# A fixed turn for TensorE between the convolution backward and the weight-gradient jobs, with reloads ahead of transposes and the spectrum's halves swapped on VectorE

## The chip, the cores and the metric

The kernel runs on one core of one Trainium2 chip. The metric is the device time of one execution in microseconds, the median of several runs. The profile is of one further execution; its clock starts at the span's first instruction. A core has a TensorE (matmuls and transposes, results to PSUM), a VectorE, a ScalarE and a GpSimd, each with its own instruction order that is fixed when the program is built, and DMA queues that are fed from the Sync, Scalar and GpSimd sequencers. An engine executes its instructions in order: one that waits holds up all behind it.

## The reference: forward and backward of two interleaved layers

The computation is the forward pass and all gradients of a stack of four residual blocks, A B A B, on 2048 tokens of width 448. A is an H3-style block (a short shift convolution of k, a product with v, a long convolution by FFT, a gate), B is a dense block with silu. Cut to what matters:

```python
def _A_ref(q, k, v, shift_k, ssm_k, ssm_D):
    k_shift = sum over t of k_pad[:, t:t+S] * shift_k[:, ks-1-t]     # 4 taps
    kv = k_shift * v
    kv_f = rfft2(kv padded to 2S);  kf_f = rfft2(ssm_k padded to 2S)
    y = irfft2(kv_f * kf_f)[:S] + kv * ssm_D
    return q * y

def _B_ref(x, w1, w2):
    h = silu(einsum("bsd,df->bsf", x, w1))            # 448 -> 1792
    return einsum("bsf,fd->bsd", h, w2)               # 1792 -> 448

x = A_q
x = x + _A_ref(_layernorm(x), A_k, A_v, ...)
x = x + _B_ref(_layernorm(x), B_w1, B_w2)
x = x + _A_ref(_layernorm(x), A_k, A_v, ...)
x = x + _B_ref(_layernorm(x), B_w1, B_w2)
# outputs: x, and the gradients of q, k, v, shift_k, ssm_k, ssm_D, w1, w2 for a given grad_out
```

Both A blocks share k, v and the convolution, so y is computed once (a prefix), and its gradient once (a suffix).

## The kernel before

The program has three parts. The prefix (to about 105 us) computes the long convolution. `Main` (to about 550 us) goes through the tokens in four chunks of 512: forward of layer 0, forward and backward of layer 1, backward of layer 0. The suffix does the backward of the convolution by FFT (stage 1, transposes `ps_tr`, a second stage `ps_s2`, products with the stored spectra, an inverse stage `ps_v`, then `ps_gK` and `ps_gkv`), and the weight gradients as "jobs": each job is 16 matmuls that accumulate `ps_d` from one loaded tile `dstat` of 512 KB. 28 jobs on activations make the gradient of w2 (`_gw2`), 28 on GH make that of w1 (`_gw1`).

A scheduler places the instructions of each engine; `issue_after` puts an instruction behind a given one. In the trace a tile's buffer number is left out (`ps_s` for `ps_s1` and `ps_s2`), and the copies of `_copy` have lines 111 (ScalarE) and 113 (VectorE).

The parts of `Main` that the change and the prediction touch:

```python
def store_turned(self, dst, tile_, c, hh, groups=((0, 4), (4, 7))):
    self.flush()
    an = self.td.tile([P, NF // 2, 4, P], BF16, name="turned", tag="S", bufs=2)
    for lo, hi in groups:
        nc.sync.dma_start_transpose(out=an[:, lo:hi]..., in_=tile_[:, lo:hi, :]...)       # L484
    self.late = lambda: nc.sync.dma_start(out=dst[...], in_=an[:, lo:hi])                 # L486
...
def slope(self, d):                                                                       # L560
    for o in range(0, 7, 2):
        self.nc.scalar.activation(d[:, o:o + n, :], d[:, o:o + n, :], ACT.Derivative_silu)
...
def ga(self, c, L, gT, dT, mid=None):
    ghT = [self.td.tile([P, NF // 2, 512], BF16, name=f"ghT{h}", tag="T", bufs=3) for h in range(2)]
    for fp in range(NF // 2):
        ps = k.psum.tile([P, 2, 512], FP32, name="ps_g", tag="mm", bufs=2)
        self.contract(ps, self.w2T, gT, 2 * fp, 2, ...)                                   # 8 matmuls, L518
        if fp == 2 and mid:
            mid()
        gh = self.ch.tile([P, 2, 512], BF16, name="ghp", tag="ghp", bufs=1)
        k.last_gh = nc.scalar.copy(gh[:], ps[:])                                          # L625
        ...
            nc.vector.tensor_tensor(out=ghT[hh][...], in0=dT[hh][1][...], in1=gh[...], op=ALU.mult)   # L630
        if fp in (3, 6):
            hh = (fp - 3) // 3
            self.store_turned(k.GH_d[L], ghT[hh], c, hh)
    return ghT
...
def load_d(self, c, hh):                                                                  # L690
    t = self.td.tile([P, NF // 2, 512], BF16, name="dTl", tag="D", bufs=3)
    k.d_load = nc.sync.dma_start(out=t[:], in_=k.DT_d[c, hh])
    return t
...
# run(), backward of layer 0
for c in range(4):
    with self.tc.issue_after(k.mid_u.ins):
        self.slope(d1)
    dT, (nb, na), (gb, gT) = ((None, d0), (None, d1)), nl, gn
    ghT = self.ga(c, 0, gT, dT, (lambda: self.slope(e0)) if c < 3 else None)
    if c < 3:
        d0, d1 = e0, self.load_d(c + 1, 1)
        if c < 2:
            e0 = self.load_d(c + 2, 0)
        gn = self.g_pre(c + 1, 0)
    self.gn(c, 0, ghT, nb, ..., na)          # 4 x 14 matmuls ps_n, then the layer norm's backward on VectorE
```

The parts of the suffix:

```python
k.M1sb = sp0.tile([P, 16, 2, P], BF16, name="M1s", tag="kk0")
with tc.high_priority():
    nc.gpsimd.dma_start(out=k.M1sb[:]..., in_=k.m1_h.ap())
...
_load_minv(k, nc.gpsimd)
for n2 in range(16):
    _fft_stage1(k, n2, k.gYb[:, n2, :], A1, psum)        # 2 matmuls ps_s, one eviction
for g in range(7):
    for i in range(16):
        nc.tensor.transpose(pt[:, i, :], A1f[:, 16 * g + i, :], k.ident[:])               # ps_tr
    _copy(nc, bal.pick(2048, dve_ns=0.53), Z[...], pt[:])

def spectrum(cp):                                         # cp: a pair of chunks of 1024 columns, 7 in all
    kk = (sp0.tile(..., name="kk_c", tag="kk0") if cp % 2 else p1.tile(..., name="kk_c", tag="kk1"))
    xsw = p1.tile([P, 2048], BF16, name="xsw_c", tag="xsw", bufs=2)
    nc.gpsimd.dma_start(out=t[0], in_=k.SPEC_d["K"][:, lo:hi])
    nc.gpsimd.dma_start(out=t[1], in_=k.SPEC_d["KV"][:, lo:hi])
    ...
    for u in range(2):
        # 2 matmuls ps_s, 512 columns each; then the eviction into Zf
    _swap_halves_dma(k, t[2], Zf, lo, hi, nc.scalar, dlo=0)      # L245, L246: two DMAs of 64 partitions

def inverse(cp, t):                                       # 4 times per cp: 2 products, 16 matmuls ps_v, an eviction
    nc.vector.tensor_tensor(out=pa[:], in0=Zf[...], in1=spec_t[:, o], op=ALU.mult)
    nc.vector.tensor_tensor(out=pb[:], in0=t[2][:, o], in1=spec_t[:, o], op=ALU.mult)
    _fft_inv_stage2_chunk(...)
...
slots = [(k.dp, "dstat", 3)]
with tc.issue_after(k.go_jobs.ins):
    _gw2(k, k.dp, range(4), slots)
slots = [(k.dp, "dstat", 3), (k.dp, "dstat", 3), (dp2, "dstat", 2), (k.dp, "dstat", 3), (dp2, "dstat", 2)]
_gw2(k, k.dp, range(4, NF), slots)
_gw1(k, dp2, slots, k.mov3, mov1)
```

The jobs are written last; the scheduler pulls their matmuls forward between those of the convolution wherever it takes TensorE to be free, so the turn in which the two kinds stand is the scheduler's.

Of the kernel before, what the change touches and what calls it, by code (L numbers as in the profile page):

```python
# [17 lines left out]
P = 128  # L18
# [188 lines left out]

def _fft_stage1(k, n2, rhs, A1, psum):
    nc = k.nc
    ps = psum.tile([P, 2, 512], FP32, name="ps_s1", **k.pt["s1"])  # L210
    for c in range(2):
        nc.tensor.matmul(ps[:, c, :D], lhsT=k.M1sb[:, n2, c, :], rhs=rhs, start=True, stop=True)
    _copy(nc, k.bal.pick(2 * D), A1[:, :, :, n2, :].rearrange("p dh c ds -> p c dh ds"), ps[:, :, :D].rearrange("p c (dh ds) -> p c dh ds", ds=4))

# [249 lines left out]
class Main:  # L464
# [98 lines left out]
    def h(self, c, L, nT, half, hold):  # L563
# [3 lines left out]
        hold.append((aT, dT))  # L567
        for ft0, n, at in ((0, 2, 1), (2, 2, 0), (4, 2, None), (6, 1, None)) if half == 0 else ((7, 1, None), (8, 2, 1), (10, 2, 0), (12, 2, None)):
# [20 lines left out]
        if L == 1:  # L589
            self.store_turned(k.A_d[1], aT, c, half)  # L590

# [24 lines left out]
    def ga(self, c, L, gT, dT, mid=None):  # L616
        nc, k = self.nc, self.k
        ghT = [self.td.tile([P, NF // 2, 512], BF16, name=f"ghT{h}", tag="T", bufs=3) for h in range(2)]
        for fp in range(NF // 2):
            ps = k.psum.tile([P, 2, 512], FP32, name="ps_g", tag="mm", bufs=2)  # L620
            self.contract(ps, self.w2T, gT, 2 * fp, 2, None if fp == 6 else (fp + 1) % 2)
            if fp == 2 and mid:
                mid()
# [3 lines left out]
            k.bal.add("dve", -0.5)  # L627
            for u in ((0, 1),) if fp != 3 else ((0,), (1,)):
# [3 lines left out]
            if fp in (3, 6):  # L632
                hh = (fp - 3) // 3
                self.store_turned(k.GH_d[L], ghT[hh], c, hh)
        return ghT
# [71 lines left out]
    def run(self):  # L707
# [21 lines left out]
        for c in range(4):  # L729
            gb, gT = self.g_pre(c, 1)  # L730
            self.h(c, 1, nT, 1, cur)
# [3 lines left out]
            self.turn_plain(c)  # L735
            if c == 3:
                d0 = self.load_d(0, 0)
                self.slope(d0)
                k.GO = k.wk.tile([P, NT, D], BF16, name="GO", tag="WA")
                with self.tc.issue_after(k.d_load.ins):  # L740
                    nc.sync.dma_start(out=k.GO[:], in_=_pm(k.grad_out[0]))
            box = []
            ghT = self.ga(c, 1, gT, cur, (lambda: box.append(self.b_pre(c + 1, 3))) if c < 3 else None)
# [5 lines left out]
            else:  # L749
                d1, e0 = self.load_d(0, 1), self.load_d(1, 0)  # L750
# [5 lines left out]
        for c in range(4):  # L756
# [3 lines left out]
            ghT = self.ga(c, 0, gT, dT, (lambda: self.slope(e0)) if c < 3 else None)  # L760
            if c < 3:
                d0, d1 = e0, self.load_d(c + 1, 1)
                if c < 2:
                    e0 = self.load_d(c + 2, 0)
                gn = self.g_pre(c + 1, 0)
            self.gn(c, 0, ghT, nb, lambda tl: self.X[:, 4 * c + tl, :], na)
            if c < 3:
                with self.tc.issue_after(k.d_load.ins):
                    nl = self.load_n(c + 1)
        self.flush()  # L770


def _job(k, ps, src, ft, mov, slot, start, stop):
    pl, tag, bufs = slot
    st = pl.tile([P, NT, P], BF16, name="dstat", tag=tag, bufs=bufs)
    k.nc.sync.dma_start(out=st[:], in_=src[:, ft, :, :])
    for t in range(NT):
        i = k.nc.tensor.matmul(ps[:, :D], lhsT=st[:, t, :], rhs=mov[:, t, :], start=start and t == 0, stop=stop and t == NT - 1)  # L778
    return i


def _gw2(k, pool, fts, slots, bufs=2):
    nc = k.nc
    for ft in fts:
        ps = k.psum.tile([P, 512], FP32, name="ps_d", tag="tr", bufs=2)
        for L, mov in ((0, k.X), (1, k.GO)):
            slot = slots.pop(0)
            slots.append(slot)
            _job(k, ps, k.A_d[L], ft, mov, slot, L == 0, L == 1)
# [5 lines left out]
def _gw1(k, pool, slots, mov3, mov1):  # L795
    nc, psum = k.nc, k.psum
    out7v = k.outs[7].rearrange("(c p) f -> p c f", p=DC)

# [9 lines left out]
    for ft in range(NF):  # L808
        ps = psum.tile([P, 512], FP32, name="ps_d", tag="tr", bufs=2)
        for L, mov in ((1, mov3), (0, mov1)):  # L810
            slot = slots.pop(0)
            slots.append(slot)
            i = _job(k, ps, k.GH_d[L], ft, mov, slot, L == 1, L == 0)
            if hold:
                with k.tc.issue_after(i.ins):
                    turn(*hold)
                hold = None
        o = pool.tile([P, D], BF16, name="dout", tag="dout", bufs=2)
        nc.vector.tensor_copy(o[:], ps[:, :D])  # L819
# [4 lines left out]
def _ssm_suffix(k):  # L824
# [7 lines left out]
    with ExitStack() as es:  # L832
        pool = lambda name: es.enter_context(tc.tile_pool(name=name, bufs=1, reuse_waits="tile"))
        sp0 = pool("sp0")
        k.M1sb = sp0.tile([P, 16, 2, P], BF16, name="M1s", tag="kk0")
        with tc.high_priority():
            nc.gpsimd.dma_start(out=k.M1sb[:].rearrange("p a c k -> p (a c k)"), in_=k.m1_h.ap())
        sp = pool("sspec")
        k.Minvsb = sp.tile([P, 16, 2, P], BF16, name="Minvs")
        dp2 = pool("dp2")  # L840
# [190 lines left out]
```

## Time and profile before

| what | value |
|---|---|
| time, median of 3 runs | 794.23 us (793.31 to 805.97) |
| span of the profiled run | 792.3 us |
| VectorE / ScalarE busy | 515.6 / 440.6 us |
| DMA moved | 183.69 MB, mean 232 GB/s |
| last matmul's start, from the trace | 784.8 us |

By stretch of the program, from the windows (busy us of each engine, the granted TensorE clock, 1.00 is full):

| stretch, us | TensorE | VectorE | ScalarE | clock | GB/s |
|---|---|---|---|---|---|
| 0 to 110, prefix | 91.21 | 81.62 | 81.76 | 0.96 | 251 |
| 110 to 365, forward and layer 1 | 248.24 | 182.26 | 172.35 | 1.00 | 223 |
| 365 to 550, end of layer 1, layer 0 backward | 160.66 | 133.69 | 113.07 | 0.94 | 242 |
| 550 to 792, convolution backward and jobs | 224.56 | 118.07 | 73.40 | 0.98 | 225 |

A line of the page's groups reads: line, engine, operation, output <- inputs, shape, count, then busy time, mean length of one in ns, and the idle time before it with what ended it. Matmuls overlap in the engine, so a mean of 350 ns is the time one takes from end to end, and not the pace. A line of a timeline is start, length, engine, source line, what, count, and in brackets the idle time ahead of it with its releaser.

### The profile page before, as it was taken

To read this page: it belongs to the slowest core of one execution; us is meant where nothing else is said; L and a number is where in the kernel's file an instruction comes from. 1 tells how busy PE (TensorE), PEld (TensorE's weight loads), DVE (VectorE), ACT (ScalarE), POOL (GpSimd) and SP (SyncE) were. 2 spreads that over 40 slices of the span, in tenths; PEclk is the share of its full clock that TensorE was granted. 3 is DMA by queue.
4 is the path that set the end of the run, shared out by engine and by line. 5 is a ranking of instruction groups with operands and counts; after the bars stand their busy time and mean duration, and the time that the engine had idled before them with its cause. 6 is when DMAs were issued, how large, how long until landed. Compare 5 with 4: busy or idle time off the path is not lost.

```text
span 792.3 us, 12745 instructions
## 1 busy us (share of the span) xinstructions
PE 724.7 (91%) x5025; PEld 381.3 (48%) x5025; DVE 515.6 (65%) x1056; ACT 440.6 (56%) x551; POOL 101.7 (13%) x169
## 2 busy tenths in 40 slices
PE   6999779999999999999978899996989998999995
PEld 4976534444444434434433343343556674545553
DVE  3789778788435978859457976985365625797110
ACT  4879867766466676876836866633536644000000
POOL 1133212222100010000000000010111022111111
PEclk9999989999999999999998999997989999999998
DMA  9359999999968869889998887995978766587660
GB/s 317 136 158 283 373 258 299 308 249 233 254 173 171 174 185 218 218 174 221 356 266 231 213 239 205 247 195 219 397 223 263 244 266 218 173 307 220 192 179 17
DMA packets 188888, 183.69 MB, mean 232 GB/s; under 512 B 135482, under 2 KB 164030, under 8 KB 187804
## 3 DMA queue, kind: packets, MB, share of 16 engines
q1 hardware_dynamic: 173664, 120.93, 59.2%
q0 software_dynamic: 12832, 53.92, 19.8%
q10 hardware_dynamic: 2332, 8.03, 3.2%
q8 instruction: 39, 0.64, 0.3%
q14 instruction: 21, 0.17, 0.1%
HBM read 76.50 MB, written 65.87 MB: 180 GB/s over the span
## 4 chain that ended last, share of the span: by engine, by line
PE 33%; DVE 21%; issue 20%; ACT 13%; DMA 8%; POOL 3%; SPq 0%; POOLq 0%; DVEq 0%; ACTq 0%
PE ps_h L518 5%; PE ps_d L778 5%; PE ps_o L598 4%; PE ps_g L518 4%; PE ps_n L666 3%; DVE dT L113 3%; DMA dTl<-DT_d 3%; ACT ghp L625 3%; DVE lb_junk L641 2%; DMA kk_c<-spec_KV 2%; DVE lb_u L652 2%; PE ps_v L232 2%; DVE ghT L630 2%; PE ps_v L233 2%; ACT na L274 2%
## 5 line engine op out<-in xcount | busy, mean ns | idle before, releaser
L778 PEld LDWEIGHTS <-dstat 128*128 128x128 bf16 x896 | 87.0, 99 | 87.4 <-issue 8.3
L518 PE MATMUL ps_g<-gT,w2T 128*128 128x512 bf16 (+1 forms) x448 | 100.7, 385 | 17.6 <-ACT ghp L625 17.0
L518 PE MATMUL ps_h<-nT,w1sb 128*128 128x512 bf16 (+1 forms) x448 | 103.9, 385 | 4.7 <-DVE dT L113 2.6
L666 PE MATMUL ps_n<-w1T,ghT 128*128 128x448 bf16 x448 | 94.2, 356 | 0.7 <-ACT lb_u L668 0.2
L598 PE MATMUL ps_o<-w2sb,aT 128*128 128x448 bf16 x448 | 90.8, 353 | 0.8 <-ACT aT L574 0.8
L778 PE MATMUL ps_d<-mov,dstat 128*128 128x448 bf16 x448 | 87.2, 352 | 0.9 <-DMA mov<-N_d 0.9
L574 ACT ACTIVATE aT<-ps_h 128x1024 bf16<-128x1024 f32 (+1 forms) x64 | 58.3, 917 | 37.6 <-PE ps_h L518 28.8
L113 DVE CAST dT<-ps_h 128x1024 bf16<-128x1024 f32 (+1 forms) x56 | 59.3, 1066 | 26.2 <-ACT aT L574 26.1
L518 PEld LDWEIGHTS <-w2T 128*128 128x128 bf16 (+1 forms) x448 | 36.3, 97 | 78.1 <-issue 47.3
L625 ACT CAST ghp<-ps_g 128x1024 bf16<-128x1024 f32 x56 | 56.5, 1008 | 30.6 <-DVE ghT L630 18.5
L518 PEld LDWEIGHTS <-w1sb 128*128 128x128 bf16 (+1 forms) x448 | 36.3, 97 | 68.3 <-issue 40.3
L666 PEld LDWEIGHTS <-ghT 128*128 128x128 bf16 x448 | 42.2, 98 | 45.4 <-issue 4.6
L598 PEld LDWEIGHTS <-aT 128*128 128x128 bf16 x448 | 42.1, 98 | 43.4 <-issue 4.3
L778 PE MATMUL ps_d<-X,dstat 128*128 128x448 bf16 x224 | 54.3, 372 | 5.1 <-DMA dstat<-A_d 5.1
L804 ACT COPY do<-ps_dt 112x512 bf16<-112x512 bf16 x14 | 8.2, 585 | 82.6 <-PE ps_dt L802 82.6
L232 PE MATMUL ps_v<-Gsb,pa 128*128 128x128 bf16 x336 | 43.2, 223 | 10.1 <-DVE Zg L113 5.8
L778 PE MATMUL ps_d<-GO,dstat 128*128 128x448 bf16 x224 | 50.0, 355 | 0.0
L233 PE MATMUL ps_v<-Gsb,pb 128*128 128x128 bf16 x336 | 42.2, 223 | 1.0 <-DVE pb L443 0.7
L819 DVE CAST dout<-ps_d 128x448 bf16<-128x448 f32 x14 | 8.7, 622 | 51.4 <-PE ps_d L778 51.4
L232 PEld LDWEIGHTS <-pa 128*128 128x128 bf16 x336 | 33.5, 100 | 11.7 <-DVE pa L442 6.3
L668 ACT ACTIVATE lb_u<-ps_n,rstd 128x448 f32<-128x448 f32 x32 | 20.2, 632 | 33.4 <-DVE X L653 12.1
L630 DVE TENSOR_TENSOR ghT<-dT,ghp 128x1024 bf16<-128x1024 bf16 (+1 forms) x32 | 19.5, 620 | 27.6 <-ACT ghp L625 27.6
(188 smaller groups left out, 1184.8 us busy)
## 6 DMA issues: line engine op xcount, KB each, us to landing
GH_d<-turned SPq DMA_DIRECT2D x16, 896.0 KB, 6.2
dstat<-A_d SPq DMA_DIRECT2D x28, 512.0 KB, 7.2
dstat<-GH_d SPq DMA_DIRECT2D x28, 512.0 KB, 3.8
A_d<-turned SPq DMA_DIRECT2D x12, 896.0 KB, 4.8
DT_d<-dT POOLq DMA_DIRECT2D x8, 896.0 KB, 6.3
dTl<-DT_d SPq DMA_DIRECT2D x8, 896.0 KB, 6.6
spec_K<-Z POOLq DMA_DIRECT2D x7, 512.0 KB, 7.5
KB<-Z POOLq DMA_DIRECT2D x14, 256.0 KB, 12.3
```

The lines of the kernel that those rows point to most:

```text
L113: eng.tensor_copy(out, in_)
L232: nc.tensor.matmul(pv[:, i, :], lhsT=pa[:, i * P:(i + 1) * P], rhs=k.Gsb[:, ga, :], start=True, stop=False)
L233: nc.tensor.matmul(pv[:, i, :], lhsT=pb[:, i * P:(i + 1) * P], rhs=k.Gsb[:, gb, :], start=False, stop=True)
L274: nc.scalar.activation(n_g[:, tl, :], src(tl), ACT.Identity, bias=nmr[:, tl:tl + 1], scale=r[:, tl:tl + 1])
L518: self.nc.tensor.matmul(ps[:, u, :], lhsT=w[lo:hi, b, f:f + P], rhs=x[lo:hi, b, :], start=(seen[u] == 1), stop=(seen[u] == ND))
L574: last = nc.scalar.activation(a, ps[:, 0:n, :], ACT.Silu)
L598: nc.tensor.matmul(po[:, :D], lhsT=aT[ft // 7][0][:, ft % 7, tl * P:(tl + 1) * P], rhs=self.w2sb[:, ft, :], start=(ft == 0), stop=(ft == N ...
L625: k.last_gh = nc.scalar.copy(gh[:], ps[:])
L630: nc.vector.tensor_tensor(out=ghT[hh][:, o:o + len(u), :], in0=dT[hh][1][:, o:o + len(u), :], in1=gh[:, u[0]:u[0] + len(u), :], op=ALU.mult)
L666: nc.tensor.matmul(pn[:, :D], lhsT=ghT[ft // 7][:, ft % 7, tl * P:(tl + 1) * P], rhs=self.w1T[:, ft, :], start=(ft == 0), stop=(ft == NF - 1))
L668: last_u = nc.scalar.activation(u0[:], pn[:, :D], ACT.Identity, scale=k.rstd[2 * L + 1][:, t:t + 1], accum_out=cp[:, tl, 0:1])
L778: i = k.nc.tensor.matmul(ps[:, :D], lhsT=st[:, t, :], rhs=mov[:, t, :], start=start and t == 0, stop=stop and t == NT - 1)
```

## The change

The change does four things.

1. In the layer backward, the reloads of `dTl` are issued inside `ga`, ahead of the transposes of the same half, where they stood behind those of the whole chunk; the slope of a reloaded tile (`mid`) is placed behind the eviction of the third `ps_g`, where it was free to stand ahead of it. The first reload (`d0`) is issued before the last chunk of layer 1 begins, and the plain transposes of the activations are done two per chunk in the first two chunks.
2. TensorE's turn in the suffix is written out. The jobs become a generator; `_in_turn` chains each group of the convolution's matmuls to the last one placed, and `weave(n)` puts n job matmuls behind it.
3. The loads around it move: M1s into the free slot of w2 by the Sync queue, a chunk earlier; Minv, ksf, gks and mov3 behind the spectrum loads of certain pairs; GO behind the reloads of chunk 0; kk_c gets two buffers of its own. The evictions of the first 12 stage-1 outputs go to ScalarE, and so do those of `_gw1`.
4. The swapped halves of the fresh spectrum are written by two VectorE copies of 64 x 1024 per chunk in place of two DMAs per pair.

No arithmetic is added or taken away. The core of the diff:

```diff
-    def ga(self, c, L, gT, dT, mid=None):
+    def ga(self, c, L, gT, dT, mid=None, loads=(None, None)):
...
-            if fp == 2 and mid:
-                mid()
             gh = self.ch.tile([P, 2, 512], BF16, name="ghp", tag="ghp", bufs=1)
             k.last_gh = nc.scalar.copy(gh[:], ps[:])
+            if fp == 2 and mid:
+                with self.tc.issue_after(k.last_gh.ins):
+                    mid()
...
             if fp in (3, 6):
                 hh = (fp - 3) // 3
+                if loads[hh]:
+                    ld.append(self.load_d(*loads[hh]))
                 self.store_turned(k.GH_d[L], ghT[hh], c, hh)
...
-            ghT = self.ga(c, 0, gT, dT, (lambda: self.slope(e0)) if c < 3 else None)
+            ghT = self.ga(c, 0, gT, dT, (lambda: self.slope(e0)) if c < 3 else None, ((c + 1, 1) if c < 3 else None, (c + 2, 0) if c < 2 else None))
...
+                    if c == 0:
+                        nc.sync.dma_start(out=k.GO[:], in_=_pm(k.grad_out[0]))
+                    if c == 2:
+                        k.M1sb = k.wk.tile([P, 16, 2, P], BF16, name="M1s", tag="WB")
+                        nc.sync.dma_start(out=k.M1sb[:].rearrange("p a c k -> p (a c k)"), in_=k.m1_h.ap())
...
+        def weave(n):
+            with _in_turn(k):
+                for _ in zip(range(n), jobs):
+                    pass
...
         for n2 in range(16):
-            _fft_stage1(k, n2, k.gYb[:, n2, :], A1, psum)
+            with _in_turn(k):
+                _fft_stage1(k, n2, k.gYb[:, n2, :], A1, psum, nc.scalar if n2 < 12 else None)
+            weave(4 if n2 < 8 else 8 if n2 < 11 else 10)
...
+                weave(3)
                 _copy(nc, bal.pick(2048, dve_ns=0.53), Z[:, 16 * g:16 * g + 16, :], pt[:])
...
-                kk = (sp0.tile([P, 2, 2048], BF16, name="kk_c", tag="kk0") if cp % 2 else p1.tile([P, 2, 2048], BF16, name="kk_c", tag="kk1"))
+                kk = p1.tile([P, 2, 2048], BF16, name="kk_c", tag="kk", bufs=2)
...
-                _swap_halves_dma(k, t[2], Zf, lo, hi, nc.scalar, dlo=0)
+                    for q in (0, 64):
+                        nc.vector.tensor_copy(t[2][q:q + 64, u * 1024:(u + 1) * 1024], Zf[64 - q:128 - q, o])
...
-                        _fft_inv_stage2_chunk(k, pa, pb, True, B1, ci, psum, cnd=cnd)
-
+                        with _in_turn(k):
+                            _fft_inv_stage2_chunk(k, pa, pb, True, B1, ci, psum, cnd=cnd)
+                        weave(5)
...
-        _gw2(k, k.dp, range(4, NF), slots)
...
-        _gw1(k, dp2, slots, k.mov3, mov1)
+        weave(2 * NF * 2 * NT)
```

## The prediction

> **What bounds the kernel now.** I read the page first, then TensorE's idle time in the trace, then the waits of the stretches in which it lies. From the page, the busy shares and the clock by slice:
>
> ```profile
> PE 724.7 (91%) x5025; PEld 381.3 (48%) x5025; DVE 515.6 (65%) x1056; ACT 440.6 (56%) x551; POOL 101.7 (13%) x169
> PEclk9999989999999999999998999997989999999998
> ```
>
> TensorE is idle for 792.3 - 724.7 = 67.6 us. The windows give 18.8 of them to the first 110 us, which the change leaves alone, and 6.8 to the 255 us after that, where matmuls run back to back. So what can be won lies in the 42 us of idle time after 365 us, and in matmuls at a slow clock. The dips of the clock row (slices 21, 27, 29) stand where TensorE had stood still. The windows show three holes, and the end for comparison:
>
> ```profile
> 410.00:420.00 10.00, 1.73 (x6) 0.57 (x5) 3.02 (x7) 4.73 (x7) 0.00 (x0) 0.75 1.02 340
> 535.00:545.00 10.00, 3.83 (x13) 1.56 (x13) 3.17 (x9) 3.15 (x5) 0.55 (x1) 0.65 0.91 340
> 570.00:580.00 10.00, 4.74 (x20) 2.12 (x19) 3.03 (x4) 2.43 (x3) 0.55 (x1) 0.78 0.97 332
> 740.00:780.00 40.00, 40.00 (x230) 21.50 (x229) 4.30 (x7) 3.51 (x6) 4.24 (x6) 1.00 0.53 152
> ```
>
> Columns: length, busy PE, PEld, DVE, ACT, POOL, clock, DMA share, GB/s. In each hole every engine is mostly idle and the DMA engines are full: waits for transfers. What TensorE waited for, 355 to 555 us, and ScalarE, 405 to 480 us (us in all, times, longest):
>
> ```profile
> PE ps_g L518 <- ACT ghp L625: 15.1, 8, 8.3
> PE ps_d L778 <- DMA dstat<-A_d: 5.1, 1, 5.1
> PE ps_s L212 <- ACT A1g L111: 1.8, 1, 1.8
> ...
> ACT dTl L560 <- DMA dTl<-DT_d: 12.1, 4, 7.5
> ```
>
> The timelines of ScalarE, then TensorE, then the Sync queue, at the largest hole:
>
> ```profile
> 415.27 1.06 ACT L560 ACTIVATE dTl<-dTl 128x1024 bf16<-128x1024 bf16 x1 [7.46 <-DMA dTl<-DT_d]
> 417.79 1.00 ACT L625 CAST ghp<-ps_g 128x1024 bf16<-128x1024 f32 x1
> ...
> 418.84 3.23 PE L518 MATMUL ps_g<-gT,w2T 128*128 128x512 bf16 x8 [8.27 <-ACT ghp L625]
> ...
> 401.90 7.20 SPq L484 DMA_TRANSPOSE turned<-ghT  x2
> 409.19 0.80 SPq L690 DMA_DIRECT2D dTl<-DT_d  x1
> ```
>
> The reload stands behind two transposes in the Sync queue; the slope (L560) stands ahead of the eviction of ps_g in ScalarE's order; so TensorE waits 8.27 us for a load that it doesn't need yet. The same chain costs 2.51 us at 444 and 1.96 us at 476. The hole at 537 is a dstat load, issued only at 535.5 behind the last GH_d store. The hole at 572 waits for kk_c, which was on its way from 558.9 to 575.4 (chain of waits) while gks, ksf, dstat and kk_c moved together at up to 425 GB/s, and then for the swapped half:
>
> ```profile
> 575.40 1.29 DVE L885 TENSOR_TENSOR pa<-Zg,kk_c 128x1024 bf16<-128x1024 bf16 x2 [5.68 <-DMA kk_c<-spec_KV]
> 581.77 0.69 DVE L886 TENSOR_TENSOR pb<-xsw_c,kk_c 128x1024 bf16<-128x1024 bf16 x1 [3.34 <-DMA xsw_c<-Zg]
> ```
>
> **What the Trainium skill says.** "TensorE: Matmul & The Clock Gate", section "What's actually happening": the array runs at half clock after a window of some 3.4 us with too little work, and returns after a busy one. The trace agrees: granted clock 0.5 for 415.1-422.0, 480.0-483.4, 538.0-548.3 and 575.6-582.4, multiples of 3.41 us, each at a hole; the 8 matmuls above take 3.23 us, 8 others 1.78. A removed hole so returns its length and half of the slow stretch behind it. "VectorE: DVE Perf Modes", section "Side-by-side: where the cycles go for N=2048 bf16": a copy within SBUF in bf16 makes four elements a cycle, with some 150 cycles fixed; by it I estimate 0.43 us for each 64x1024 swap. No copy of that form is in this trace; the nearest, skb<-sk_all with a strided read, takes 1.10. "DMA: Bandwidth & Descriptors", section "Issuing engines are not separate DMA queues": transfers from all issuers share the same 16 engines. It agrees: the swap's 256 KB take 3.0 to 9.6 us, by what else moves.
>
> **The change part by part.** No matmul is added or removed: 5,025 before and after. The pace from start to start is 0.19 us for 448 columns (50 ps_o in 9.69), 0.215 for 512, 0.056 for 128 (27 ps_tr in 1.68).
>
> (a) Slope reloads. In the new order the loads for the next chunks stand ahead of the second transpose of each half, and the slope comes behind the eviction of the third ps_g. Holes of layer 0, as excess over the pace: 8.4 + 2.7 + 0.8 + 0.5 + 2.1 + 0.6 + 0.5 = 15.6 us; half of the slow clock's 3.1 and 3.4 us: 3.3. Together 18.9. Not all comes back: VectorE is busy 97.4 of the 118 us from 418 to 536. Per chunk it has 4 x 5.4 (the lb, G, gy, gYb rows: 2 x 0.70, 2 x 0.17, 0.69, 0.68, 0.76, 2 x 0.38, 2 x 0.39) + 4.9 for ghT = 26.5 us, against some 24.5 on TensorE. VectorE is also idle for nearly all of the first hole, so those 8 to 9 us are real; of the rest I count a third. Gain: 12. The early load of d0 takes perhaps 1 of 2.4 us of gaps at 369-386.
>
> (b) The convolution backward in fixed turn. The last ps_n ends at 527.2, the last matmul starts at 784.8: 257.6 us. The work in it by pace: 835 ps_d x 0.189 = 157.8; ps_s 32 x 0.189 + 28 x 0.215 = 12.1; 744 of 128 columns (ps_tr 112, ps_v 448, ps_gK 128, ps_dt 56) x 0.0565 = 42.0; ps_gkv 6.1; ps_sk and ps_r 5.4; about 80 changes from ps_d to another kind at 0.05 = 4. Sum 227.4, so 30 us are waits and half clock: 2.0 + 5.3 + 3.0 (clock) at 534-548, 5.4 + 2.3 at 572-582, 1.9 at ps_r, 1.1 at mov1, 0.7 + 0.5 + 1.7 in small ones, and some 6 in many tiny ones.
> In the new order 2 ps_s and 4 to 10 ps_d take turns, 106 ps_d before the first ps_tr (79 before), and the evictions of the first 12 stage-1 outputs are on ScalarE, not behind VectorE's late layer norm. M1s is loaded a chunk earlier and Minv later, which frees the DMA engines just when the last ghT transposes gate the next dstat. kk_c no longer shares a slot with M1s, so the first two pairs can come some 20 us before their use.
> What stays: the third ft's dstat is needed 8 x (0.38 + 0.76 + 0.05) = 9.5 us after the last ps_n, and came 15 us after it before; without M1s and Minv I expect 7 to 11, a wait of 0 to 2. mov1 takes 7.8 us against two jobs of 3: 1 to 2. Turn changes rise to some 97: +1. Sum of what stays, with tiny ones: 8. Gain 22.
>
> (c) The swap. 14 DMA pairs go (3.7 MB), 28 VectorE copies come: 28 x 0.43 = 12 us. For a pair of chunks (cp) VectorE then has 8 x 0.69 + 4 x 0.43 = 7.2 us and ScalarE 6 evictions x 1.02 = 6.1, while TensorE has 2 x (0.43 + 0.38) + 4 x (0.90 + 0.95) + turns = 9.7. The copies lie beside TensorE's work: they cost nothing, and the gain is counted in (b).
>
> (d) The end (mov jobs, 7.5 us after the last matmul) is unchanged; dout's eviction moves to ScalarE at 0.54 for VectorE's 0.62. 0.
>
> Sum: 12 + 1 + 22 = 35 us; 794.2 - 35 = 759. As new waits are likelier than forgotten gains I take 761.
>
> **The rivals.** First: the fixed turn makes TensorE wait in place, since a dstat that is late now holds up the spectrum too. Against it: a job of 16 takes 4.5 to 9 us with its neighbours, a dstat lands in 7.2 at the median with three to five slots open. For it: kk_c, dstat, ksf, gks, mov3 and Minv all fall into the 70 us of the spectrum, some 270 GB/s where 244 moved before. If it holds, 8 to 15 us of (b) are lost: 770 to 776.
> Second: VectorE becomes the bound. In layer 0 it nearly is; if only the first hole pays, (a) shrinks to 8: 765. If the swap runs at one element a cycle (1.1 us), a cp costs VectorE 10, just over TensorE's 9.7: again 3 to 5 us.
> Third: GO (1.8 MB), moved into layer 0, and two early plain turns delay reloads or transposes there, so that a hole only moves: 5 us. The gb reload has slack: issued at 279, used at 313.
> Fourth, upward: if VectorE's idle time in layer 0 also goes and tiny waits shrink, 752.
>
> **Range and chances.** Rivals one and two together make some 775, the best case 751: range 751 to 775. Over 2% faster means below 778.3, which asks for 16 of the 35 us; the first hole and the kk_c hole with their clock alone bring nearly that. Faster 0.91, same 0.07, slower 0.02.
>
> **What would show it.** (a): no wait of ps_g for ghp over 1 us, no half clock near 410, the last ps_n 11 to 15 us earlier. (b): last ps_n to last matmul some 235 us, no slow clock in between, no wait for kk_c. (c): swaps at 0.43 us, no idle TensorE behind them. Wrong if ps_d waits for dstat<-A_d in many places, if a slope load again stops ScalarE for over 3 us, or if VectorE is over 90% busy in the spectrum.

## The result and the profile after

The changed kernel takes 768.89 us (median of 4 runs, 765.53 to 771.57), the kernel before, run beside it, 795.23 us. The ratio is 0.9675, 95% interval 0.9621 to 0.9728: 3.25% faster. A second time it was 770.33 us, ratio 0.9754 (0.9716 to 0.9793). The prediction was 761 us, 751 to 775: the time lies in the range, 8 us above the point.

Three marks in the trace, each the start of a matmul, cut the program so that each part of the change can be read by itself: the first `ps_g`, the last `ps_n`, and the last matmul.

| stretch, us | before | after | difference | predicted |
|---|---|---|---|---|
| start to first ps_g (nothing of the prediction) | 232.1 | 234.5 | +2.4 | 0 |
| first ps_g to last ps_n: layers | 294.9 | 284.9 | -10.1 | -13 |
| last ps_n to last matmul: convolution backward and jobs | 257.7 | 242.8 | -14.9 | -22 |
| last matmul to the end | 7.6 | 7.6 | 0.0 | 0 |

The sum is -22.6, from a span of 792.3 to one of 769.8. I call the second stretch "the layers" and the third "the suffix" from here on. The first differs from run to run: 230.4 to 240.6 in the fourteen traces of this study. The two highest values (240.5 and 240.6) come from traces with a wait near 145, where a transposing DMA of aT, 1.5 us in the changed kernel's own trace, took 9.3 and 9.2; the same kernel shows both values, so it is not an effect of the change.

Busy shares and clock by slice, from the page of the changed kernel:

```profile
PE 719.6 (93%) x5025; PEld 382.3 (50%) x5025; DVE 510.3 (66%) x1061; ACT 457.6 (59%) x574; POOL 102.5 (13%) x169
PEclk9999879999999999999999999999999998999999
```

TensorE's idle time fell from 67.6 to 50.2 us, and the three dips that stood behind the middle of the row are gone. One new one stands at 635 to 654 us (the 34th digit). The windows of the changed kernel (length, busy PE, PEld, DVE, ACT, POOL, clock, DMA share, GB/s) show the layers' last stretch, the spectrum, and the two stretches behind it:

```profile
410.00:520.00 110.00, 103.48 (x529) 44.28 (x528) 91.50 (x252) 73.39 (x104) 2.17 (x4) 1.00 1.07 263
562.00:623.00 61.00, 59.67 (x624) 42.23 (x625) 45.27 (x82) 39.49 (x44) 9.29 (x18) 1.00 0.72 264
623.00:646.00 23.00, 20.08 (x183) 14.19 (x181) 2.60 (x3) 8.25 (x9) 5.98 (x9) 0.85 0.74 261
646.00:668.00 22.00, 19.65 (x308) 11.56 (x307) 10.30 (x25) 8.13 (x10) 5.97 (x11) 1.00 0.67 218
```

The spectrum has 1.3 us of idle TensorE in 61. The 45 us behind it have 5.3 us and a slow clock: a part of the suffix where the prediction had seen no large wait. TensorE's waits from 519 to 680 us, the first lines:

```profile
PE ps_gK L981 <- ACT gK L111: 2.9, 1, 2.9
PE ps_sk L1030 <- issue: 2.4, 1, 2.4
PE ps_v L233 <- DVE pb L942: 1.1, 2, 0.8
```

No wait for kk_c, none for a dstat. And in the layers, from 355 to 520 us, the answer to the 15.1 us of before:

```profile
PE ps_g L518 <- ACT ghp L626: 5.4, 12, 1.5
```

### The profile page after: what moved, and what is told of

It is laid out like the page before. It is cut to its first block, busy times and chain, and to the rows that moved or that the text cites. A ratio compares the mean times of both kernels' runs of the same rounds, so it can differ in the third digit from the quotient of the medians.

```text
span 769.8 us, 12724 instructions
## 1 busy us (share of the span) xinstructions
PE 719.6 (93%) x5025; PEld 382.3 (50%) x5025; DVE 510.3 (66%) x1061; ACT 457.6 (59%) x574; POOL 102.5 (13%) x169
## 4 chain that ended last, share of the span: by engine, by line
PE 38%; DVE 25%; issue 15%; ACT 11%; DMA 8%; POOL 3%; SPq 0%; POOLq 0%; DVEq 0%; ACTq 0%
PE ps_d L808 8%; PE ps_o L600 7%; PE ps_h L518 6%; DVE lb_junk L647 3%; DVE dT L113 3%; ACT ghp L626 3%; DVE ghT L634 3%; DVE lb_u L658 2%; DMA turned<-ghT 2%; PE ps_v L233 2%; PE ps_v L232 2%; PE ps_n L672 2%; DVE ln_st L260 2%; DVE lb_u L687 2%; ACT na L274 2%
## 5 line engine op out<-in xcount | busy, mean ns | idle before, releaser
L808 PEld LDWEIGHTS <-dstat 128*128 128x128 bf16 x896 | 85.4, 98 | 73.6 <-issue 1.8
L672 PE MATMUL ps_n<-w1T,ghT 128*128 128x448 bf16 x448 | 92.6, 353 | 0.9 <-DVE ghT L634 0.4
L808 PE MATMUL ps_d<-X,dstat 128*128 128x448 bf16 x224 | 52.7, 359 | 0.1
L852 ACT CAST dout<-ps_d 128x448 bf16<-128x448 f32 x14 | 7.5, 533 | 58.6 <-PE ps_d L808 58.6
L232 PEld LDWEIGHTS <-pa 128*128 128x128 bf16 x336 | 33.6, 100 | 10.1 <-DVE pa L442 6.5
L233 PEld LDWEIGHTS <-pb 128*128 128x128 bf16 x336 | 33.3, 100 | 9.0 <-DVE pb L443 4.3
```

What stands on the lines that cost most here:

```text
L232: nc.tensor.matmul(pv[:, i, :], lhsT=pa[:, i * P:(i + 1) * P], rhs=k.Gsb[:, ga, :], start=True, stop=False)
L233: nc.tensor.matmul(pv[:, i, :], lhsT=pb[:, i * P:(i + 1) * P], rhs=k.Gsb[:, gb, :], start=False, stop=True)
L672: nc.tensor.matmul(pn[:, :D], lhsT=ghT[ft // 7][:, ft % 7, tl * P:(tl + 1) * P], rhs=self.w1T[:, ft, :], start=(ft == 0), stop=(ft == NF - 1))
```

## The experiments

Twelve kernels ran, each for five rounds beside the kernel before. The times of one chip are compared by their ratio to the kernel before on it; the two stretches come from one trace each.

| kernel | ratio (95%) | median us | layers | suffix |
|---|---|---|---|---|
| before | 1 | | 294.9 | 257.7 |
| changed | 0.9675 (0.9621, 0.9728) | 768.9 | 284.9 | 242.8 |
| changed again | 0.9754 (0.9716, 0.9793) | 770.3 | 284.7 | 242.3 |
| scheduler's turn, copies | 0.9802 (0.9768, 0.9835) | 773.8 | 284.2 | 246.0 |
| scheduler's turn, DMA swap | 0.9847 (0.9816, 0.9878) | 779.1 | 284.4 | 251.9 |
| fixed turn, DMA swap | 0.9926 (0.9896, 0.9957) | 786.3 | 284.2 | 260.1 |
| each swap twice | 0.9815 (0.9775, 0.9855) | 776.9 | 284.4 | 251.3 |
| reloads and slope undone | 0.9825 (0.9795, 0.9856) | 776.3 | 290.7 | 244.0 |
| only the slope undone | 0.9777 (0.9747, 0.9807) | 773.0 | 291.5 | 241.3 |
| only the loads' place undone | 0.9718 (0.9675, 0.9761) | 767.3 | 284.5 | 240.8 |
| kernel before, slope moved alone | 0.9893 (0.9849, 0.9938) | 780.3 | 285.3 | 252.2 |
| changed, ps_sk broken up | 0.9671 (0.9633, 0.9709) | 763.2 | 284.5 | 237.2 |
| changed, kx_s loaded late | 0.9764 (0.9723, 0.9805) | 771.0 | 284.4 | 244.8 |
| changed, four gK and ps_sk broken up | 0.9642 (0.9613, 0.9671) | 762.4 | 284.4 | 235.5 |

Where a kernel leaves the layers alone they take 284.2 to 284.9 us, so a difference of 1 us in that column already means something. The suffix is less steady: five traces with the suffix of the changed kernel (changed, changed again, and the three with other layers) have 240.8 to 244.0 us. A difference of some 3 us there, from one trace each, is likely at best.

### The changed kernel again

> The changed kernel once more, as the base of the others on the same chip. Theory: 768.9 us again within 3 us, the wait of ps_gK for the eviction of gK (2.9 us, then 6.8 us at half clock) and the pause of 2.4 us inside ps_sk come again at the same place, so they belong to the kernel and not to one execution. Rival: they are chance, and a second profile lacks one of them; the time is then 763 to 766.

The theory held. Its layers and suffix agree with the first trace to 0.5 us, and both waits came again, but at another price: ps_gK waits 2.1 us, with 3.4 us at half clock behind it, where it was 2.9 with 6.8; the pause in the ps_sk is 2.2 us, with 3.4 us at half clock behind it, where it was 2.4 with none. What differs most is the first stretch (240.5 us for 234.5), so I compare stretches and not spans.

### The layers: which half of part (a) paid?

The first of four runs puts the reloads (that of d0 too) and the slope back, as they were before:

```diff
+            if fp == 2 and mid:
+                mid()
             k.last_gh = nc.scalar.copy(gh[:], ps[:])
-            if fp == 2 and mid:
-                with self.tc.issue_after(k.last_gh.ins):
-                    mid()
...
-                if loads[hh]:
-                    ld.append(self.load_d(*loads[hh]))
...
+                d0, d1 = e0, self.load_d(c + 1, 1)
+                if c < 2:
+                    e0 = self.load_d(c + 2, 0)
```

> The changed kernel with the reloads behind the chunk's transposes again, the slope free to stand ahead of the eviction, and the first reload after the last chunk's output, as before; the suffix stays as changed. Theory: the hole of 8 us at 410, with its half clock, and the two of 2 us come back: 779 us, 10 more, and the last ps_n 10 us later. Rival: with GO out of the way of the Sync queue the reloads come in time in the old place as well, and only 3 us come back: 772.

Measured: the layers take 290.7 us, 5.8 more, between theory and rival. The holes are back: ps_g waits for ghp at 412.5 (3.7 us), 441.5 (2.4) and 473.5 (2.3), with 3.4 us at half clock behind each of the last two. Next, the slope alone is free to stand ahead of the eviction; the early reloads stay:

```diff
+            if fp == 2 and mid:
+                mid()
...
-            if fp == 2 and mid:
-                with self.tc.issue_after(k.last_gh.ins):
-                    mid()
```

> The changed kernel, only the slope of a reloaded tile is free again to stand ahead of the third eviction of ps_g; the reloads stay ahead of the transposes. First ps_g to last ps_n was 294.9 us before, 284.8 with the change, 290.7 with both of reloads and slope undone. Theory: the place of the loads is what counts, as a load that has landed lets the slope run at once in either place; 285-286.5 us. Rival: the order on ScalarE is what counts: 288-291 us, with ps_g waiting over 2 us for ghp again.

The rival held: 291.5 us, no better than with both undone. ScalarE's timeline at the first hole of this kernel:

```profile
406.84 1.06 ACT L560 ACTIVATE dTl<-dTl 128x1024 bf16<-128x1024 bf16 x1 [6.91 <-DMA dTl<-DT_d]
...
408.41 4.40 ACT L560 ACTIVATE dTl<-dTl 128x1024 bf16<-128x1024 bf16 x5
...
413.32 1.57 ACT L560 ACTIVATE dTl<-dTl 128x1024 bf16<-128x1024 bf16 x2
414.79 1.00 ACT L628 CAST ghp<-ps_g 128x1024 bf16<-128x1024 f32 x1
```

and of the changed kernel:

```profile
405.40 3.46 ACT L560 ACTIVATE dTl<-dTl 128x1024 bf16<-128x1024 bf16 x4
...
411.26 1.01 ACT L626 CAST ghp<-ps_g 128x1024 bf16<-128x1024 f32 x1 [0.69 <-PE ps_g L518]
...
417.93 3.47 ACT L560 ACTIVATE dTl<-dTl 128x1024 bf16<-128x1024 bf16 x4
```

With the slope free, all eight of its instructions (two tiles of four) stand ahead of the eviction, and the first of them waits 6.91 us for a load that was issued at 400.24, ahead of the last transpose, and was there only by 406.8. In the changed kernel the second four come behind the third eviction and wait for nothing. The opposite run leaves the slope behind the eviction and puts only the loads back behind the transposes:

```diff
-                if loads[hh]:
-                    ld.append(self.load_d(*loads[hh]))
...
+                d0, d1 = e0, self.load_d(c + 1, 1)
+                if c < 2:
+                    e0 = self.load_d(c + 2, 0)
```

> The changed kernel, only the reloads of dTl stand again behind the transposes of the whole chunk; the slope stays behind the third eviction of ps_g. First ps_g to last ps_n was 284.8 us with the change, 291.5 with only the slope undone, 290.7 with both undone. Theory: ScalarE's order is the cause, and a slope behind the eviction has some 10 us of slack, so a later load costs little: 284.5 to 286.5. Rival: each of the two is needed, and a slope that waits for a late load stops the fourth eviction in place of the third: 288 to 291.

284.5 us: the place of the loads is worth nothing here. ScalarE waits 0.3 us in all for a reload, between 400 and 525. Last, the kernel before with the slope's order as its only edit:

```diff
-            if fp == 2 and mid:
-                mid()
             k.last_gh = nc.scalar.copy(gh[:], ps[:])
+            if fp == 2 and mid:
+                with self.tc.issue_after(k.last_gh.ins):
+                    mid()
```

> The kernel before with one edit alone: the slope of a reloaded tile stands behind the third eviction of ps_g. First ps_g to last ps_n was 294.9 us in the kernel before, 284.8 in the changed one. Theory: this one order on ScalarE carries most of the layers' gain: 286 to 289 us, the 8.3 us wait of ps_g for ghp falls under 2.5 us. Rival: in the kernel before the load is still later (behind more transposes in the Sync queue), so the slope stops the fourth eviction instead: 291 to 295.

285.3 us, 9.6 of the 10.1 that the whole change wins in the layers, and more than the theory had. The wait of ps_g for ghp, 15.1 us with 8.3 as its longest in the kernel before, is here:

```profile
PE ps_g L518 <- ACT ghp L623: 6.1, 12, 1.5
```

Taken together: one order on ScalarE is nearly the whole of part (a). Its 5.8 to 6.6 us when undone in the changed kernel are less than the 9.6 when done in the kernel before; the first hole, a wait of 8.3 us there, is 3.7 with both undone in the changed one. Something else in the change makes it shorter, perhaps the plain transposes that left the Sync queue; that wasn't tried by itself, and with the slope behind the eviction it plays no part.

In this kernel the suffix is shorter as well, 252.2 for 257.7 us, though nothing in it was edited: the wait for the dstat is 3.2 us for 5.1, and 10.2 us are at half clock for 17.1. The scheduler may also place the jobs otherwise when anything ahead of them moves; how much that has in it is not shown.

### The suffix: the turn and the swap, two by two

First the swap by DMA again, in the fixed turn:

```diff
-                    for q in (0, 64):
-                        nc.vector.tensor_copy(t[2][q:q + 64, u * 1024:(u + 1) * 1024], Zf[64 - q:128 - q, o])
+                _swap_halves_dma(k, t[2], Zf, lo, hi, nc.scalar, dlo=0)
```

> The changed kernel with the swapped halves moved by DMA from the ScalarE queue, as before, and the rest as changed. Theory: the copies lie beside TensorE's work and a pair has 10 us of lead, so in a fixed turn with kk_c in time the DMA would do nearly as well: +1 to +3 us, from the first pair, whose swap has no lead, and from 3.7 MB more on the DMA engines; 770 to 772. Rival: TensorE in fixed turn can't step past a late half, each of the seven pairs waits 1 to 2 us: 779 or more.

260.1 us, 17.3 more than with the copies: slower than the suffix of the kernel before, and my theory fell. The rival had the size, though not the form: four halves make TensorE wait, for 1.2 to 4.5 us. Of this kernel, TensorE's first wait of 519 to 680 us, then the lines of the tile xsw_c that tell what its readers waited for and how long a half took from issue to landing:

```profile
PE ps_v L233 <- DVE pb L941: 13.4, 4, 4.5
```

```profile
  DMA xsw_c<-Zg: 27.2, 5
...
DMA to landing us min/median/max: 3.0/6.7/12.8
```

VectorE is idle for 27.2 us because of late halves, and TensorE for 13.4, where it was 1.1. Behind the holes the clock is at half for three times 3.4 us, of which half is lost. 12.3 + 5.1 = 17.4 us, the size of the difference; what else differs further on is small (a pause in the ps_sk, below, of 3.9 us for 2.4). The copy of the changed kernel, by its tile:

```profile
L930 DVE COPY xsw_c<-Zg x28: 420/422/425, 559.2 to 610.2; 64x1024 bf16<-64x1024 bf16 x28
```

Now the turn left to the scheduler, with the copies:

```diff
 def _in_turn(k):
-    bb = k.nc.cur_bb.bb
-    with ExitStack() as es:
-        if k.tail is not None:
-            es.enter_context(k.tc.issue_after(k.tail))
...
+    yield
...
-            with _in_turn(k):
-                for _ in zip(range(n), jobs):
-                    pass
+            if n == 2 * NF * 2 * NT:                      # all jobs written last, as before
+                ...
```

> The changed kernel with its turn left to the scheduler: the jobs' matmuls are written last, as before, all else of the change stays (loads moved, swaps on VectorE, evictions on ScalarE, reloads). Theory: the turn is what fills TensorE while VectorE and ScalarE follow, worth 6 to 8 of the 15 us that the suffix gained; 775 to 777 us, with waits of ps_s, ps_v and ps_gkv for evictions. Rival: the loads (M1s, Minv, kk_c slots) and the swap had made the gain, and the turn is worth 0 to 2 us; 769 to 771.

246.0 us: the turn is worth 3.2 us, less than the theory and more than the rival had. By the times on the same chip it is 3.4 (773.8 for 770.3 us), but the two intervals overlap, so the gain is likely and its size rough. It is also a net figure. By the windows of the suffix, TensorE is busy in this kernel for 237.0 us and never at half clock; in the changed one, with the same matmuls, for 233.5, of which 6.8 are at half clock and 3.4 so lost. The turn saves some 7 us of TensorE's time and gives half of it back to a slow clock that the end of the suffix brings (below). And the fourth corner, both edits together:

> The changed kernel with the turn of jobs and convolution left to the scheduler and the halves swapped by DMA: the fourth corner beside the changed kernel (242.8 us from last ps_n to last matmul), turn by the scheduler with copies (246.0) and fixed turn with DMA (260.1). Theory: the fixed turn makes the late half a wait of TensorE; where the scheduler places more job matmuls between or other ones, a late half costs less, so this one lies at 248-254 us, under the fixed turn with DMA. Rival: both parts add up, +3.2 for the turn on top of 260.1: 261-265 us; the DMA costs the same 17 us in either turn.

251.9 us, as the theory had it. The four corners of the suffix:

| | swap by DMA | swap by copies | copies win |
|---|---|---|---|
| scheduler's turn | 251.9 | 246.0 | 5.9 |
| fixed turn | 260.1 | 242.8 | 17.3 |
| fixed turn wins | -8.2 | 3.2 | |

The two parts don't add up: the DMA costs 17.3 us in one turn and 5.9 in the other, and this difference is far over the spread of the traces. Of the fourth corner, by the tile xsw_c, what its readers waited for, who waited for them, and the time from issue to landing:

```profile
  DMA xsw_c<-Zg: 31.8, 7
...
  PE ps_v L233: 10.0, 3
...
DMA to landing us min/median/max: 3.2/7.3/13.1
```

A half is as late in the scheduler's turn, and VectorE waits as long; but TensorE only waits 10.0 us for 13.4, with two slow stretches of 3.4 us behind it for three. The fixed turn loses more in the end of the suffix, by its wait for gK (2.7 us), its pause in the ps_sk (3.9) and the slow clock behind each. Against this stands what it saves of TensorE's time; in all it is 8.2 us worse here. With the fixed turn but without the copies the suffix would have been slower than that of the kernel before. What the moved loads bring can't be read from the remaining 5.8 us (257.7 to 251.9), as the kernel before with the slope alone also comes to 252.2.

How much room have the copies? Each was made twice:

```diff
-                    for q in (0, 64):
+                    for q in (0, 64, 0, 64):
```

> The changed kernel with each half-swap copied twice: 28 more VectorE copies of 64 x 1024, 28 x 0.42 = 11.8 us more work for VectorE in the spectrum, nothing else changed. Theory: the copies lie beside TensorE's work and cost nothing until VectorE is the slower: of the 9.7 us that TensorE needs for a pair of chunks VectorE had 7.2 and has 8.9 now; last ps_n to last matmul 242-245 us. Rival: the copy is on the path from the spectrum to its product, so doubling it costs its whole length or half of it: 248-255 us.

251.3 us, 8.5 more, in the range of the rival. The trace is of an execution of 785.7 us, slower than the other five (773.0 to 780.0 us), mostly in its first stretch; by the ratios of the others the loss is 0.6 to 1.4%, or 5 to 11 us, so its size is rough. The trace puts it in one place. VectorE's timeline at the front of the spectrum in this kernel, and TensorE's first wait from 519 to 690 us:

```profile
565.01 7.21 DVE L930 COPY xsw_c<-Zg 64x1024 bf16<-64x1024 bf16 x16
572.26 0.69 DVE L941 TENSOR_TENSOR pa<-Zg,kk_c 128x1024 bf16<-128x1024 bf16 x1
```

```profile
PE ps_v L232 <- DVE pa L941: 5.7, 1, 5.7
```

Sixteen copies, those of two pairs, stand ahead of the first product; TensorE waits 5.7 us and then runs 6.8 us at half clock, 3.4 lost. The other 40 copies find room beside TensorE: from 580 to 640 us it is busy for all of the 60 us, at full clock. So the copies are hidden where the spectrum runs, and on the path at its front. In the changed kernel the scheduler put a product between the first copies (two copies, pa, two copies, pb), and of their 3.5 us at most 1.6 show, as the small waits of ps_v.

### The end of the suffix: where the other 7 us went

The two waits at the head of the list above were not in the prediction. gK's eviction (ScalarE) and its matmul (TensorE), from the two timelines of the changed kernel:

```profile
636.61 1.01 ACT L111 CAST gK<-ps_gK 112x1024 bf16<-112x1024 f32 x1 [6.34 <-DMA out_dram<-gK]
```

```profile
637.68 1.87 PE L981 MATMUL ps_gK<-Minvs,A1g 128*112 128x128 bf16 x16 [2.92 <-ACT gK L111]
```

gK has two buffers; the third can't be written before the first is stored. The clock is at half from 636.8 to 643.6, another 3.4 us lost. Then the ps_sk, also TensorE's timeline:

```profile
660.87 2.69 PE L1030 MATMUL ps_sk<-kx_s,gks 128*32 128x128 bf16 x177
665.91 1.28 PE L1030 MATMUL ps_sk<-kx_s,gks 128*32 128x128 bf16 x47 [2.35 <-issue]
```

224 short matmuls, 15 ns from start to start, and a pause after the 177th in which TensorE waited for nothing that this view shows. It is in all eight traces of a fixed turn in which they stand in one block, each time after the 177th, for 2.2 to 4.1 us. In the scheduler's turn 168 of them stand together; one of its four kernels, the one with copies, pauses 2.2 us two matmuls behind that block, and the other three don't. Both causes were taken away together:

```diff
-            gK = p2.tile([DC, S], BF16, name="gK", tag="gK", bufs=2)
+            gK = p2.tile([DC, S], BF16, name="gK", tag="gK", bufs=4)      # and the other tiles of this tag
...
-        weave(16)
+        weave(12)
         for g in range(4):
+          if g:
+            weave(4)
           with _in_turn(k):                                              # 64 ps_sk, 32 in the last group
```

> The changed kernel with two small edits in its end: gK gets four buffers for two, and the ps_sk are placed in groups with 4 job matmuls between them, where 224 stood in one block. Theory: the gK eviction waits for the store of the buffer before it (6.34 us on ScalarE, 2.9 us on TensorE, then some 3.4 us lost to half clock), and the block of short ps_sk holds a pause of 2.4 us that goes when it is broken up. Then last ps_n to last matmul shrinks from 242.8 to 234-238 us, the ratio to the kernel before from 0.9675-0.9754 to about 0.963-0.967. Rival: the store is late because the DMA engines are full (kx_s, 1.8 MB), so something else waits in its place (ps_gkv, a dstat), and the pause moves to another place: 241-244 us, time within 2 us of the changed kernel.

235.5 us: 7.3 us gone, and no new wait. The windows of this kernel for the same two stretches, against 20.08 at clock 0.85 and 19.65 of the changed one:

```profile
623.00:646.00 23.00, 23.00 (x216) 15.27 (x214) 5.25 (x7) 11.21 (x12) 7.67 (x12) 1.00 0.89 306
646.00:668.00 22.00, 22.00 (x318) 12.05 (x316) 8.87 (x29) 5.97 (x9) 4.84 (x9) 1.00 0.74 252
```

With 762.4 us, ratio 0.9642 (0.9613 to 0.9671), it is the lowest ratio of all. Its interval lies below that of the second run of the changed kernel and overlaps that of the first (0.9621 to 0.9728), so by times the step is likely rather than certain; by the trace the two waits are gone. The second half of the edit alone:

> The changed kernel, only the block of 224 ps_sk is broken up into four groups with 4 job matmuls between. Last ps_n to last matmul was 242.8 us, and 235.5 with this and four gK buffers together. Theory: this part carries the pause of 2.4 us in the block and no more: 239.5 to 241 us, the wait of ps_gK (2.9 us and half clock) stays. Rival: the pause is a fetch of instructions that falls every so many instructions and only moves: 242 to 243.5.

237.2 us, better than both had it. The pause is gone, and the wait of ps_gK is still there with 2.3 us; but this time no slow clock followed it. The kernel with late loads, which has the same wait (2.4 us, no slow clock) and the block of ps_sk whole, took 240.8 on the same chip; so the block costs 3.6 us, its pause of 2.4 and the slow clock that followed there from 661.1 to 664.5, of which half is lost. For gK some 1.7 us are left (237.2 to 235.5, one trace each) when the clock holds, and 1.7 to 3.4 more when it drops.

What the pause is, no run tests, but the packets of the traces point to it. In each of the nine pauses TensorE goes on 1.3 to 1.5 us after the end of a fetch of 16 KB of instructions through a DMA queue: in the changed kernel the pause lasts from 663.56 to 665.91 and the fetch from 663.51 to 664.45. Where the fetch starts 1.2 to 1.7 us into the pause, the pause is 3.6 to 4.1 us long. With the groups such fetches come as well, and nothing waits. So the likely reading is the first half of the rival: TensorE ran out of instructions in a block of very short ones. The second half, that the pause only moves, is refuted.

Why is gK's store late? The load of kx_s (2.1 MB) is issued as the first gK comes out. In the last run it waits for the last store:

```diff
-        nc.scalar.dma_start(out=kx[:, 3:19, :], in_=k_pm)                  # ahead of the loop over gK
...
+        with tc.issue_after(gst.ins):                                      # behind its last store
+            nc.gpsimd.dma_start(out=kx[:, 3:19, :], in_=k_pm)
```

> The changed kernel, only the load of kx_s (2.1 MB) is issued behind the last store of gK, where it was issued as the first gK came out. Theory: the store of gK lands late because it shares the DMA engines with kx_s; without it the stores take 3.5 to 5 us, ScalarE's wait for the buffer falls from 6.3 to under 3.5 us, TensorE's 2.9 us and the half clock behind it go: last ps_n to last matmul 237 to 240 us, for 242.8. Rival: dstat and mov fill the engines as well, and the store takes as long: 242 to 244; or kx_s then comes too late for ps_sk: 245 and more.

The cause of the late store is shown. From issue to landing of the gK stores, in the changed kernel and then in this one:

```profile
DMA to landing us min/median/max: 3.4/5.8/9.0
DMA to landing us min/median/max: 3.6/4.2/5.5
```

ScalarE no longer waits for a store of gK, nor does ps_gK wait. But the time isn't won, 244.8 us. The late load, which the edit also moves from ScalarE's queue to GpSimd's, now stands ahead of the store of gD, 0.9 KB, which lands after 13.7 us for 3.3 and whose buffer gkv needs next. ScalarE's line of waits from 630 to 668 us, and TensorE's from 519 to 690:

```profile
ACT gkv L1009 <- DMA out_dram<-gD: 4.5, 1, 4.5
```

```profile
PE ps_gkv L1006 <- ACT gkv L1009: 4.8, 3, 3.7
```

A wait was exchanged for another, and the pause in the ps_sk is longer too (3.6 us for 2.4); two more buffers are the better cure.

## Why the prediction was right, and where it was off

**(a), layers: gain 12 + 1 predicted, 10.1 measured; the mechanism half right.** The hole was read rightly: TensorE waited for a slope that ScalarE ran ahead of an eviction. No ps_g wait over 1.5 us is left, and the clock is full from 410 to 520. The step counted "the loads for the next chunks stand ahead of the second transpose of each half, and the slope comes behind the eviction" as one cause. The runs separate them: the slope's place brings 9.6 us alone, that of the loads nothing. That VectorE is nearly the bound, so that only a third of the rest comes back, was right: it is busy 91.5 of 110 us there, and what ScalarE's evictions still wait for is VectorE's ghT.

**(b), suffix: gain 22 predicted, 14.9 measured; the waits were rightly named, but their sum was too large.** The prediction counted 835 matmuls ps_d behind the last ps_n of the kernel before; its trace has 867. The missing 32 are 6.0 us at the prediction's own pace, just what it listed as "some 6 in many tiny ones". So 24 us were waits and half clock and not 30, and with the prediction's own 8 us of what stays the gain would have been 16.

The second step that failed is what stays. The size of 8 us was near: at that pace the suffix of 242.8 us leaves some 10. The causes were others. The prediction listed the dstat of the third ft (0 to 2), mov1 (1 to 2) and turn changes; in fact dstat was never waited for and mov cost 0.2. What did cost were gK's two buffers (2.9 us and 3.4 of slow clock) and the block of ps_sk (2.4). With both mended the suffix takes 235.5 us; that this is the predicted 235 is luck, as the work was put too low and what stays too high. As TensorE's wait the profile of before shows neither, since the scheduler had placed other work there. But the same trace has ScalarE waiting 4.4 us and VectorE 5.3 us for the store of a gK, and the chain that ended last runs through such a store for 4.6 us at 650.5: a fixed turn makes waits of TensorE out of them.

**(b), what it is to be credited to.** "The convolution backward in fixed turn" was the heading, and the turn alone is worth some 3 us with the copies and -8.2 without. The largest single step in the suffix is the swap.

**(c), the swap: 0.43 us a copy predicted, 0.422 measured.** The estimate from the Trainium skill, "VectorE: DVE Perf Modes", section "Side-by-side: where the cycles go for N=2048 bf16", is confirmed for copies of 64 partitions that move to other partitions. "They cost nothing" holds within the spectrum. "The gain is counted in (b)" hid how large it was. The prediction shows one late half (3.34 us); in that same profile VectorE waits five times for one, 11.5 us in all, though no wait of TensorE is put down to them.

**(d), the tail:** 0 predicted, 0.0 measured.

**The rivals.** The first, that a fixed turn makes TensorE wait in place, is true, but not for the dstat that I had named: the swapped half is what is late, and the change takes that away in the same step. The second came true only in part, as VectorE takes the rest of the gain in the layers. The third: no reload was delayed enough to matter. The fourth, upward, did not come.

By the traces the gain was 12.4 us too large in the sum: 7.1 in (b), 2.9 in (a), and 2.4 by which the first stretch came out longer by chance. Two things made the time look nearer: the profiled execution of the changed kernel was the slowest of four, 2.7 us over their median, and 1.8 us had been put on top of the sum. So 7.9 us are left, from 761 to 768.9.

## What to carry to other kernels

A fixed turn trades the scheduler's luck for exactness, and is only as good as its latest input: before you fix it, take the inputs with an uncertain time (here a DMA of 3 to 13 us) off the path, even by work on another engine that has room. When a load that is late stops an engine, ask first whether the instruction that waits for it must stand where it does; moving it behind the urgent one can bring all that an earlier load was meant to bring. And a stretch that the scheduler filled with other work hides its own waits: look in the code for buffers that are too few for their stores before you take the filling away.

## What the hardware showed that I hadn't expected

A hole in TensorE's work is not always followed by a slow clock. The Trainium skill, "TensorE: Matmul & The Clock Gate", section "What's actually happening", speaks of a window of activity; in these traces the pause of 2.4 us in the ps_sk was followed by no slow clock in the changed kernel and by 3.4 us of it in the one with late loads. The wait for gK was followed by 6.8 us of it after 2.9 us, by 3.4 after 2.1 in the same kernel's second trace, and by none after 2.3 in the one with the ps_sk broken up; one of 3.7 us by none (ps_gkv in the kernel with the late kx_s). So the same wait costs up to 3.4 us more or nothing, and a single trace can't price it.

And 224 matmuls of 15 ns each don't run through: after 177 TensorE pauses for 2.2 to 4.1 us, until shortly after a fetch of instructions has landed, and groups of 64 with a few long ones between don't show it.
